# The last two experts' second products left for the routing, with one expert's middle units parked in DRAM

## The chip, the cores and the metric

One core of one Trainium2 chip. TensorE multiplies, VectorE, ScalarE and GpSimd work on elements, SP issues most transfers; each engine takes its instructions in the order in which the program gives them, and waits on semaphores for the others. The metric is the time of one launch in device microseconds.

## The reference

The reference runs a windowed attention, a layer of four weighted experts and a layer of eight experts with a fixed capacity, over 1536 tokens of 512 features.

```python
def _moe_ref(x, domain_probs, w1, w2):          # E = 4, F = 1024
    p = domain_probs / (domain_probs.sum(-1, keepdims=True) + 1e-09)
    ...
    for e in range(E):
        h = np.maximum(x @ w1[e], 0.0)
        out += p[:, e:e + 1] * (h @ w2[e])

def _moe2_ref(x, w_gate, w1, w2):               # E = 8, cap = N // E = 192
    logits = x @ w_gate
    flat = logits.flatten()
    order = np.argsort(-flat)
    ...
    for idx in order:
        tok, e = (int(idx) // E, int(idx) % E)
        if assigned[tok] >= 0 or counts[e] >= cap:
            continue
        assigned[tok] = e
        counts[e] += 1
    ...
    for e in range(E):
        mask = assigned == e
        h = np.maximum(x[mask] @ w1[e], 0.0)
        out[mask] = h @ w2[e]
```

A token's expert in the second layer depends on the rank of its logit among all tokens of that expert, so ranks must be exact over all 12288 logits.

## The kernel before

Tokens come in 12 blocks of 128. Every float32 operand is split into two float16 parts, high and low, and a product is three float16 products. The hidden layer stands with its units on partitions, so a first product (`g1`, 12 matmuls a step) needs no transpose after it.

The program has four stages. `phase1` (0 to 352 us) does the attention and experts 0 and 1, in an order written out as a list (`ORDER1`). `phase3` does expert 2 ("mid") and the first product of expert 3 ("last"), unit by unit: unit m holds blocks 2m and 2m+1. For each unit, `a00` to `a31` are the eight steps of mid's first product and `a40` to `a71` those of the last expert's; `r` is the relu out of the accumulators, `h` the high part and `l` the low part of the result. Mid's parts go into one pair of buffers (`HH`), the last expert's over the tokens themselves (`xTall`, high) and into `hl3` (low), which both stay until the routing. `s00` to `s17` are mid's second products for units 0 to 4 (`KEEP = 5`), added into `y` by `add`.

The logits of the second layer are not taken from the finished `y`. `norm`, `sc`, `xh`, `xl`, `row` split a block of `y` as far as it is summed, SP transposes it, and `log_mm` adds to its product with the gate the products of kept hidden units with `gv`, which is W2 times the gate (made by `gate_of`: `turn` transposes W2, `prod` multiplies, `gate` closes). So an expert's second product may be done after the logits. Here this holds for the last expert in all blocks and for mid in blocks 10 and 11.

Ranking runs beside it, block by block (`lm`, `lo`, `rr`, `cm`, `rc`, `ct`, `rk`): `rank_rows` turns the block's logits into rows, `compare` (VectorE) compares each of the 8 experts' logits of this block with all blocks up to it, `row_count` (ScalarE) sums along rows, `count` (TensorE) along columns, `ranked` puts the two together. In blocks 8 to 11 two experts are summed on VectorE instead of ScalarE. Ties within the block are taken off by a second instruction with the mask `notbefore`.

Second products left over are cut into fills of two matmuls each (`defer`): 2 blocks of mid and 12 of the last expert, 14 x 12 = 168 fills. `side_step`, called after every third fill, does what follows a finished block: add, square, scale, high, low, and the write of the row to DRAM (`rows`). `FILLS` puts 75 of them into phase 3; the routing (`route`), a chain of 30 hops between VectorE and TensorE, calls `HOPS[i]` fills ahead of hop i; what is left runs after it, three fills to a step of `pump`, which loads, scales and splits the second layer's weights.

The order of phase 3 comes from due times: `TIMES3` within a unit, plus `PERIOD3` for each unit, `RANK` and `FILLS`, sorted (`ORDER3` is empty). The second layer gathers rows of 192 tokens an expert from DRAM (`gather`, an indirect transfer of GpSimd), transposes them (`gather_T`) and runs the experts.

```python
            while fills:
                fill(3)
                s.pump(1)
            while s.side:
                s.side_step()
                s.pump(1)
            W = s.finish(2, 0)
            big.close()
```

## Time and profile before

| | us |
|---|---|
| median of 3 runs (870.05 to 871.53) | 871.49 |
| the profiled execution | 871.92 |
| its span, first to last instruction | 870.1 |
| TensorE busy | 769.3 |
| VectorE busy | 612.3 |
| ScalarE busy | 494.4 |
| GpSimd busy | 244.7 |

Times in the rows are microseconds from the start of the span. The page gives each engine's busy tenths in 40 slices; a stretch can be asked for with the busy time of each engine in it, and with the granted clock of TensorE as a share of 2.4 GHz (1.00 is 2.4, 0.50 is 1.2). A matmul's duration includes its way through the array, so matmuls that follow each other overlap: what one costs is the distance from its start to the next start.

### The profile page before, as it was taken

Reading aid. Unit: us, or ns where it says so; the run is one execution under the profiler, and the core shown is the slowest. Engines: PE = TensorE matmul, PEld = TensorE weight load, DVE = VectorE, ACT = ScalarE, POOL = GpSimd, SP = SyncE. Lnnn points to the kernel's source line nnn. Section 1 sums busy time; section 2 is a strip of 40 time slices with the busy share of each in tenths; the row PEclk is TensorE's granted clock in tenths of the full one; section 3 lists DMA queues with packets and bytes.
Section 4 is the critical chain, followed back from the end, with each engine's and each line's share of the span. In section 5 each row is a group of like instructions: output and inputs, shape, how many; then the busy total and the mean of one; then the engine's idle time right before and its main releaser. Section 6 shows DMA issues by size and latency. Waiting matters only on the chain. (4 is left out here: it accounts for less than half of the span.)

```text
span 870.1 us, 21221 instructions
## 1 busy us (share of the span) xinstructions
PE 769.3 (88%) x8660; PEld 591.3 (68%) x8664; DVE 612.3 (70%) x1545; ACT 494.4 (57%) x989; POOL 244.7 (28%) x287
## 2 busy tenths in 40 slices
PE   3688999999999999999999998889899147998996
PEld 3567767777776767768778685745344047898996
DVE  5998988767663543436668788999777545797790
...
PEclk9699999999999999999999999989999568999999
...
GB/s 281 254 193 131 150 157 160 127 133 59 98 111 171 98 68 80 109 98 14 26 2 26 14 24 23 48 69 1 183 37 39 132 221 336 257 256 331 177 38 38
DMA packets 191425, 103.75 MB, mean 119 GB/s; under 512 B 162272, under 2 KB 162272, under 8 KB 191328
## 3 DMA queue, kind: packets, MB, share of 16 engines
...
q8 instruction: 68, 1.11, 0.5%
...
## 5 line engine op out<-in xcount | busy, mean ns | idle before, releaser
L873 PEld LDWEIGHTS <-w 128*128 128x128 f16 x3456 | 246.5, 98 | 37.4 <-issue 5.4
L873 PE MATMUL pH<-xT,w 128*128 128x128 f16 (+1 forms) x3168 | 249.1, 234 | 3.7 <-ACT H L847 2.7
L884 PE MATMUL pY<-w,hh 128*128 128x512 f16 x544 | 161.7, 379 | 0.0
L884 PE MATMUL pY<-w,hl 128*128 128x512 f16 x272 | 103.1, 379 | 0.2 <-DVE hl L1425 0.2
L1017 ACT ACTIVATE Cj<-C 128x128 bf16<-128x128 bf16 (+11 forms) x88 | 75.3, 855 | 42.5 <-DVE C L1004 41.6
L1278 PEld LDWEIGHTS <-w 128*128 128x128 f16 x768 | 66.7, 102 | 37.0 <-DMA xg<-g 23.4
L847 ACT ACTIVATE H<-pH 128x512 f32<-128x512 f32 (+1 forms) x82 | 45.4, 559 | 61.9 <-PE pH L873 48.8
L1004 DVE TENSOR_SCALAR C<-w,Lg 128x1024 bf16<-128x1024 f32 (+7 forms) x112 | 72.2, 661 | 3.7 <-PE pw L1023 1.8
L1278 PE MATMUL pH<-xg,w 128*128 128x192 f16 x528 | 51.8, 259 | 22.0 <-DMA xg<-g 19.5
L884 PEld LDWEIGHTS <-hh 128*128 128x128 f16 x544 | 47.0, 98 | 33.6
L1298 PE MATMUL pR<-hh,w 128*128 128x192 f16 x512 | 64.9, 246 | 0.0
L1298 PEld LDWEIGHTS <-w 128*128 128x128 f16 x768 | 63.4, 98 | 1.9 <-issue 1.8
L1298 PE MATMUL pR<-hl,w 128*128 128x192 f16 x256 | 63.0, 246 | 0.0
L1049 PE MATMUL pY<-w,xT 128*128 128x512 f16 x192 | 60.4, 389 | 0.0
L569 POOL TENSOR_SCALAR hh<-H 128x512 f16<-128x512 f32 x40 | 28.5, 713 | 101.2 <-ACT H L847 76.0
L749 ACT ACTIVATE t<-pS,mx,ec 128x256 f32<-128x256 f32 (+1 forms) x96 | 51.6, 542 | 2.2
L764 POOL TENSOR_TENSOR pp<-t,pp 128x512 f16<-128x512 f32 (+1 forms) x34 | 39.8, 1175 | 44.4 <-ACT pp L567 36.0
L481 DVE SCALAR_TENSOR_TENSOR w<-w,wsr,w 128x1024 f16<-128x1024 f32 x32 | 40.3, 1279 | 13.4 <-ACT w L567 13.4
L1425 POOL TENSOR_TENSOR hl<-H,hh 128x512 f16<-128x512 f32 x26 | 32.9, 1267 | 56.4 <-DVE hh L571 31.7
L884 PEld LDWEIGHTS <-hl 128*128 128x128 f16 x272 | 26.5, 98 | 32.7 <-DVE hl L1425 0.7
L481 DVE SCALAR_TENSOR_TENSOR w<-raw,wsr,w 128x1024 f16<-128x1024 f32 x32 | 40.2, 1279 | 7.5 <-ACT w L567 7.2
L1049 PE MATMUL pY<-w,hl 128*128 128x512 f16 x112 | 44.2, 395 | 0.0
...
## 6 DMA issues: line engine op xcount, KB each, us to landing
...
rows<-xs SPq DMA_DIRECT2D x12, 260.0 KB, 2.7
x<-in_k_dram SPq DMA_DIRECT2D x12, 256.0 KB, 3.5
x<-in_q_dram SPq DMA_DIRECT2D x12, 256.0 KB, 4.3
```

Source lines behind the costliest of these rows:

```text
L481: V.scalar_tensor_tensor(l, r[:, d2], sc, h, op0=OP.mult, op1=OP.subtract)
L749: s.nc.scalar.activation(t[:, hh], ps[:, hh], AF.Exp, bias=mx[:, 1, hh:hh + 1], scale=e[:, 0:1], accum_out=s.SU[j][:, 2 * g + hh:2 * g + h ...
L764: (G if eng == "G" else V).tensor_sub(pl[:, x], t, ph[:, x])
L847: s.nc.scalar.activation(H, ps, AF.Relu, scale=HS)
L873: nc.tensor.matmul(o[f], w[:, d, 128 * (f0 + f):128 * (f0 + f) + 128], x[:, :, c], start=(d == 0 and i == 0), stop=(d == 3 and i == 2))
L884: nc.tensor.matmul(py, l[:, f], w[:, f], start=(f == 0 and i == 0), stop=(f == 7 and i == 2))
L1004: V.tensor_scalar(C[:, 8 * i:8 * i + n], x[:, :n, e], l, None, op0=OP.is_ge)
L1017: s.nc.scalar.activation(x, C, AF.Copy, accum_out=s.AC[j][:, 1, e:e + 1])
L1049: nc.tensor.matmul(py, a[:, f], w[:, f], start=(n == 0), stop=(n == 23))
L1278: nc.tensor.matmul(ps[0][:, f % 2], w[:, d, 128 * f:128 * f + 128], xg[:, :, c], start=(k == 0), stop=(k == 11))
L1298: nc.tensor.matmul(ps[0][:, d % 2], w[:, f, 128 * d:128 * d + 128], h[:, f], start=(k == 0), stop=(k == 23))
L1425: (nc.gpsimd if eng == "G" else nc.vector).tensor_sub(x[1], P.pop((e, j, c)), x[0])
```

## The change

Mid's second products leave phase 3 altogether: `second`, `s00` to `s17` and `add` go, and all 12 blocks of mid become fills, after the 12 of the last expert (288 fills). Since mid's buffers hold one unit only, `spill` writes each unit's two parts to DRAM, and when the last expert's fills of a block are done, the block's parts are read back over its own places in `xTall` and `hl3`. `log_mm` takes mid's hidden units for every block. A block's row steps now follow mid's fills, and the logits' split takes `y` with experts 0 and 1 alone.

In the ranking, `compare` covers the j blocks before the own one; the own block is one more instruction with the mask `lower`, whose result stands in `C` as block j and is counted like the others. The fixed part of the rank comes from `behind`. The accumulators are cleared in blocks 8 to 11 only. The shares `pe` are made at once for 12 blocks (`shares`). `FILLS` has 96 entries, `HOPS` 101 fills instead of 88, `junk` has a buffer of its own, and the whole order of phase 3, with the engine of each relu and part, is written out in `ORDER3` (775 steps; 18 of 48 relus, 29 of 48 low parts and 7 of 48 high parts on VectorE, 30 relus and 28 high parts on ScalarE).

```diff
-ORDER3 = """""".split()
-PERIOD3 = 35.0
+ORDER3 = """
+    norm0 sc0 a00 pump pump.1 mturn0 a01 pump.2 mturn1 a10 pump.3 pump.4 pump.5 pump.6 r0/A mprod0 a11 r1/V a20 mturn2
+    mturn3 mprod1 a21 mturn4 xh0/V h0/G pump.7 l0/G pump.8 pump.9 a30 mturn5 a31 xl0 r2/V h1/V a40 row0 l1/G r3/A
+    pump.10 pump.11 pump.12 pump.13 h2/G pump.14 mprod2 norm1 a41 pump.15 a50 pump.16 mturn6 a51 pump.17 sc1 mturn7
+    l2/G mprod3 xh1/V a60 a61 mgate start h3/A turn0 l3/G turn1 prod0 turn2 r4/A turn3 turn4 a70 a71 xl1 r5/A h4/A
...
+    xh1.1/A a70.1 r4.1/V a71.1 h4.1/A r5.1/V xl1.1 l4.1/V rc5.1 row1.1 a00.2 fill.3 rc6.1 h5.1/G norm0.2 ct5.1 r6.1/V
+    l5.1/G a01.2 sp.1 h6.1/G a10.2 r7.1/V fill.4 l6.1/V sc0.2 h7.1/G l7.1/V lm.2 a11.2 xh0.2/A lo.2 ct6.1 rr.2 r0.2/V
+    xl0.2 r1.2/A cm0.2 lm.3 fill.5 rc0.2 cm7.1 ct0.2 rc7.1 cm1.2 fill.6 ct7.1 h1.2/G row0.2 cm2.2 fill.7 cm3.2 norm1.2
+    a20.2 rk.1 rc1.2 lo.3 rc2.2 ct1.2 ct2.2 fill.8 fill.9 cm5.2 cm4.2 a21.2 rc3.2 sc1.2 rc4.2 ct3.2 h0.2/G rc5.2 a30.2
+    l0.2/V cm6.2 ct4.2 r2.2/A ct5.2 l1.2/V rc6.2 fill.10 cm7.2 rr.3 ct6.2 a31.2 cm0.3 cm1.3 r3.2/V rc7.2 rc0.3 ct7.2
...
+    rc2.11 rk.10 ct1.11 ct2.11 cm3.11 ct3.11 cm4.11 cm5.11 rc4.11 rc5.11 cm6.11 fill.74 fill.75 fill.76 fill.77
+    fill.78 fill.79 ct4.11 ct5.11 rc6.11 fill.80 fill.81 fill.82 fill.83 ct6.11 fill.84 fill.85 fill.86 fill.87 cm7.11
+    fill.88 fill.89 ct7.11 fill.90 rk.11 fill.91 fill.92 fill.93 fill.94 fill.95
+""".split()
+PERIOD3 = 29.0
...
-KEEP = 5
...
-HOPS = [0, 1, 3, 1, 7, 0, 3, 1, 7, 1, 3, 1, 7, 1, 3, 1, 7, 1, 3, 1, 7, 1, 4, 1, 7, 0, 3, 2, 4, 7]
+HOPS = [0, 1, 4, 1, 8, 1, 4, 1, 8, 1, 4, 1, 8, 1, 4, 1, 8, 1, 4, 1, 8, 1, 4, 1, 8, 1, 4, 1, 4, 7]
...
         V.tensor_copy(s.identh, s.identb)
-        s.notbefore = c.tile([128, 128], BF, name="notbefore")
-        V.tensor_scalar(s.notbefore, d0, 0.0, None, op0=OP.is_le)
+        s.lower = c.tile([128, 128], BF, name="lower")
+        V.tensor_scalar(s.lower, d0, 0.0, None, op0=OP.is_gt)
+        s.behind = c.tile([128, 1], F32, name="behind")
+        V.tensor_scalar(s.behind, d0[:, 0:1], -1.0, 127.0, op0=OP.mult, op1=OP.add)
         s.upper = c.tile([128, 128], BF, name="upper")
...
         xs, inv = s.XN.pop(j)
-        xt = s.xp.tile([128, 8, 128], F16, name="xt3" if j == s.NB - 2 else "xt2", bufs=1)
+        xt = s.xp.tile([128, 8, 128], F16, name=f"xt{2 + j % 2}", bufs=1)
         s.nc.sync.dma_start_transpose(xt, xs[:, 0:1024])
...
         s.AC[j] = s.sm.tile([128, 3, s.E2], F32, name="acc")
-        nc.vector.memset(s.AC[j][:, 2], 0.0)
+        if j >= 8:
+            nc.vector.memset(s.AC[j], 0.0)
         c = 64 + 128 * (j % 2)
-        s.PC[j] = s.pw[:, c:c + 8 * j].rearrange("p (a b) -> p a b", b=8) if j else None
+        s.PC[j] = s.pw[:, c:c + 8 * j + 8].rearrange("p (a b) -> p a b", b=8)
...
         C = s.Cs[j, e] = s.rk.tile([128, s.NB, 128], BF, name="C", bufs=3)
+        acc = s.on_dve(j, e)
         for i, x in enumerate(s.LR):
-            n = min(j + 1 - 8 * i, 8)
-            if s.on_dve(j, e):
+            n = min(j - 8 * i, 8)
+            if n < 1:
+                continue
+            if acc:
                 V.tensor_scalar(C[:, 8 * i:8 * i + n], x[:, :n, e], l, 0.0, op0=OP.is_ge, op1=OP.add,
...
-
-        jk = s.rk.tile([128, 128], BF, name="jk")
-        V.scalar_tensor_tensor(jk, s.LRof[j][:, e], l, s.notbefore, op0=OP.is_equal, op1=OP.mult,
-                               accum_out=s.AC[j][:, 0, e:e + 1])
+        kw = dict(accum_out=s.AC[j][:, 0, e:e + 1]) if acc else {}
+        V.scalar_tensor_tensor(C[:, j], s.LRof[j][:, e], l, s.lower, op0=OP.is_ge, op1=OP.mult, **kw)
...
         C = s.Cs.pop((j, e))
-        for jj in range(j):
+        for jj in range(j + 1):
             s.nc.tensor.matmul(s.PC[j][:, jj, e:e + 1], C[:, jj], s.ones[:, 0:1], start=True, stop=True)
...
         acc = s.AC.pop(j)
-        V.scalar_tensor_tensor(R[:, j], acc[:, 1], late, acc[:, 0], op0=OP.add, op1=OP.subtract)
-        V.tensor_add(R[:, j], R[:, j], acc[:, 2])
-        if j:
-            V.tensor_sub(R[:, :j], R[:, :j], s.PC.pop(j))
+        V.scalar_tensor_tensor(R[:, j], acc[:, 1], late, s.behind.to_broadcast([128, 8]), op0=OP.add, op1=OP.add)
+        if j >= 8:
+            V.tensor_add(acc[:, 0], acc[:, 0], acc[:, 2])
+            V.tensor_add(R[:, j], R[:, j], acc[:, 0])
+        V.tensor_sub(R[:, :j + 1], R[:, :j + 1], s.PC.pop(j))
         s.prefer(j)
+    def shares(s, e, W):
+        pe = s.cp.tile([128, s.NB], F32, name=f"pe_{e}")
+        s.nc.vector.scalar_tensor_tensor(pe, s.p[:, :, e], W[4], s.tsc, op0=OP.mult, op1=OP.mult)
+        s.kpe[e] = {j: pe[:, j:j + 1] for j in range(s.NB)}
...
             py = s.pys[e, j]
-            h, l = s.kept[e][j]
+            h, l = s.xTall[:, j], s.hl3[:, j]
             for n in (2 * k, 2 * k + 1):
...
             if k == 11:
-                s.side.append([add] if e < s.E1 - 1 else [add, norm])
+                s.side.append([add, norm] if e < s.E1 - 1 else [add])
+                if e == s.E1 - 1:
+                    for p, x in enumerate((s.xTall, s.hl3)):
+                        nc.sync.dma_start(x[:, j], s.spill[p, j])
...
-        NB, V, G, E = s.NB, s.nc.vector, s.nc.gpsimd, s.E2
-        ev, B, HH, PE, W3 = {}, {}, {}, {}, []
+        nc, NB, V, G, E = s.nc, s.NB, s.nc.vector, s.nc.gpsimd, s.E2
+        ev, B, HH, W3 = {}, {}, {}, []
         mid = s.E1 - 2
...
                     HH[m] = [s.hp.tile([128, 8, 2, 128], F16, name=x, bufs=1) for x in ("hh", "hl")]
-                    if m >= KEEP:
-                        pe = s.pe_of(mid, W[4], 2 * m, 2 * m + 2)
-                        for b in range(2):
-                            s.kept[mid][2 * m + b] = [x[:, :, b] for x in HH[m]]
-                            s.kpe[mid][2 * m + b] = pe[:, b:b + 1]
+                    for b in range(2):
+                        s.kept[mid][2 * m + b] = [x[:, :, b] for x in HH[m]]
                 h, l = [y[:, 2 * k:2 * k + 2] for y in HH[m]]
...
-        def second(m, b, i):
-            j = 2 * m + b
-            if m not in PE:
-                PE[m] = s.pe_of(mid, W[4], 2 * m, 2 * m + 2)
-            if i == 0:
-                B[j] = s.g2(W, HH[m][0][:, :, b], HH[m][1][:, :, b], j, PE[m][:, b:b + 1], False)
-            B[j][0][i]()
+        def spill(m):
+            for p in range(2):
+                nc.sync.dma_start(s.spill[p, 2 * m:2 * m + 2].rearrange("b q f t -> q f b t"), HH[m][p])
...
         W2 = s.gate_of(mid, W)
+        s.shares(mid, W)
...
                 at(f"r{k}", m, T, relu, m, k, after=rp + [(f"l{k - 2}", m) if k > 1 else (f"l{k + 6}", m - 1), (f"r{k - 1}", m)], eng="A")
-                at(f"h{k}", m, T, hid, m, k, 0, after=[(f"r{k}", m), ("a71", m) if k > 3 else ("s17", m - 1)], eng="G")
+                at(f"h{k}", m, T, hid, m, k, 0, after=[(f"r{k}", m)] + ([("a71", m)] if k > 3 else [("lm", 2 * m - 2), ("lm", 2 * m - 1), ("sp", m - 1)]), eng="G")
                 at(f"l{k}", m, T, hid, m, k, 1, after=[(f"h{k}", m)], eng="G" if k > 3 else "V")
-            y = [(f"l{k}", m) for k in range(4)]
+            at("sp", m, T, spill, m, after=[(f"l{k}", m) for k in range(4)])
             for b in range(2):
                 j = 2 * m + b
-                d = "" if m < KEEP else "d"
-                for i in range(8 if m < KEEP else 0):
-                    at(f"s{b}{i}", m, T, second, m, b, i, after=y + [(f"add{b}", m - 1)])
-                    y = [(f"s{b}{i}", m)]
-                if m < KEEP:
-                    at(f"add{b}", m, T, lambda j=j: B.pop(j)[1](), after=y)
-                xs = (("row1", m - 1) if b else ("row1", m - 2)) if d else ("row0", m) if b else \
-                    ("drow0", m + 1) if m + 1 == KEEP else ("row1", m - 1)
-                at(f"{d}norm{b}", m, T, norm, j, after=[(f"add{b}", m), xs])
-                at(f"{d}sc{b}", m, T, put, j, s.rows_scale, after=[(f"{d}norm{b}", m)])
-                at(f"{d}xh{b}", m, T, lambda e, j=j: s.rows_hi(s.XN[j], e), after=[(f"{d}sc{b}", m)], eng="G")
-                at(f"{d}xl{b}", m, T, put, j, s.rows_lo, after=[(f"{d}xh{b}", m)])
-                at(f"{d}row{b}", m, T, s.log_rows, j,
-                   after=[(f"{d}xl{b}", m), ("drow0" if d and not b else "lm", j - 2 if d else j - 1)])
+                at(f"norm{b}", m, T, norm, j, after=[("row0", m) if b else ("row1", m - 1)])
+                at(f"sc{b}", m, T, put, j, s.rows_scale, after=[(f"norm{b}", m)])
+                at(f"xh{b}", m, T, lambda e, j=j: s.rows_hi(s.XN[j], e), after=[(f"sc{b}", m)], eng="G")
+                at(f"xl{b}", m, T, put, j, s.rows_lo, after=[(f"xh{b}", m)])
+                at(f"row{b}", m, T, s.log_rows, j, after=[(f"xl{b}", m), ("lm", j - 2)])
         cs = []
...
             m, T = r // 2, PERIOD3 * (r // 2 + 1)
-            at("lm", r, T + RANK[4 * r + 0], s.log_mm, r, after=[(f"row{r % 2}", m), (f"drow{r % 2}", m), ("lo", r - 1), ("gate", 0)] + [(f"l{k}", m) for k in range(4, 8)])
+            at("lm", r, T + RANK[4 * r + 0], s.log_mm, r, after=[(f"row{r % 2}", m), ("lo", r - 1), ("gate", 0)] + [(f"l{k}", m) for k in range(8)])
             at("lo", r, T + RANK[4 * r + 0], s.log_out, r, after=[("lm", r)])
...
         at("gate", 0, 0, gate, after=[("prod3", 0)])
-        m = NB // 2 - 1
-        f = [("add0", m), ("add1", m), ("add0", m - 1), ("add1", m - 1)] + [(f"l{k}", m) for k in range(8)]
         for i, t in enumerate(FILLS):
-            ev["fill", i] = [PERIOD3 * m + t, fill, f + [("fill", i - 1)]]
+            j = i // 12
+            ev["fill", i] = [PERIOD3 * (NB // 2 - 1) + t, fill, [("fill", i - 1), ("gate", 0), (f"xl{j % 2}", j // 2), ("lm", j)]]
         for i, t in enumerate(PUMPS3):
...
             rows = dr.tile([s.N, ROW], F16, name="rows")
+            s.spill = dr.tile([2, NB, 128, 8, 128], F16, name="spill")
             s.rows = rows[:]
...
                     s.rk = pool(ph, "rk", 1, **re)
+                    s.shares(last, W)
                     for j in range(NB):
-                        pe = s.cp.tile([128, 1], F32, name=f"pe3_{j}")
-                        nc.vector.scalar_tensor_tensor(pe, s.p[:, j, last:], W[4], s.tsc[:, j:j + 1],
-                                                       op0=OP.mult, op1=OP.mult)
-                        s.kpe[last][j] = pe
                         s.kept[last][j] = (s.xTall[:, j], s.hl3[:, j])
-                    for j in range(2 * KEEP, NB):
-                        fills.extend(s.defer(last - 1, Wm, j))
                     for j in range(NB):
                         fills.extend(s.defer(last, W, j))
+                    for j in range(NB):
+                        fills.extend(s.defer(last - 1, Wm, j))
                 s.phase3(W, w1, open_rk, fill)
...
                 if s.nfill == 16:
-                    s.junk = s.y[:, 0:2].bitcast(F16).rearrange("p a (b f) -> p (a b) f", f=512)
+                    s.junk = pool(hb, "junk1", 1, **re).tile([128, 4, 512], F16, name="junk")
                 s.pump(1)
```

## Rows read from the trace of the kernel before

**Rows 1.** The page's 40 slices: TensorE's busy tenths and clock.
```profile
PE   3688999999999999999999998889899147998996
PEclk9699999999999999999999999989999568999999
```

**Rows 2.** Busy by stretch: length, PE, PEld, DVE, ACT, POOL, clock, DMA, GB/s.
```profile
458.30:496.40 38.10, 36.61 (x383) 28.26 (x381) 31.19 (x100) 21.65 (x50) 12.18 (x14) 1.00 0.08 15
496.40:534.40 38.00, 36.94 (x403) 28.72 (x401) 32.76 (x94) 23.69 (x49) 13.07 (x15) 1.00 0.17 22
562.10:617.50 55.40, 46.47 (x501) 25.32 (x498) 52.65 (x163) 33.22 (x53) 8.91 (x16) 0.94 0.17 57
617.50:678.70 61.20, 55.33 (x399) 24.27 (x397) 44.37 (x155) 22.92 (x44) 1.03 (x10) 0.95 0.20 76
678.70:707.20 28.50, 0.51 (x4) 0.29 (x5) 17.34 (x29) 16.40 (x20) 4.25 (x4) 0.50 0.55 151
```

**Rows 3.** Timeline, TensorE, routing: start, us, line, operation, count.
```profile
639.75 0.59 PE L1049 MATMUL pY<-w,xT 128*128 128x512 f16 x2
...
640.40 0.59 PE L1049 MATMUL pY<-w,xT 128*128 128x512 f16 x2
```

**Rows 4.** Timeline of TensorE in unit 2: logit, count and first products.
```profile
426.43 0.17 PE L957 MATMUL pq<-gv,hl 128*128 128x8 f16 x1
426.46 0.16 PE L1023 MATMUL pw<-ones,C 128*128 128x1 bf16 x1
426.48 1.47 PE L873 MATMUL pH<-xT,w 128*128 128x256 f16 x12
427.79 0.17 PE L1023 MATMUL pw<-ones,C 128*128 128x1 bf16 x1
```

**Rows 5.** Groups by line and shape, 380 to 617: count, busy us, mean ns.
```profile
L1004 DVE TENSOR_SCALAR C<-w,Lg 128x1024 bf16<-128x1024 f32 x32 | 25.3, 790 | 0.1
...
L1004 DVE TENSOR_SCALAR C<-w,Lg 128x512 bf16<-128x512 f32 x14 | 7.6, 543 | 0.0
...
L1007 DVE DVE_READ_ACCUMULATOR jk<-w,Lg,notbefore 128x1 f32 x96 | 7.6, 79 | 0.0
...
L891 DVE SCALAR_TENSOR_TENSOR y<-pY,pe,y 128x512 f32<-128x512 f32 x10 | 7.5, 745 | 21.0 <-PE pY L884 20.9 <-PE pw L1023 0.2
...
L567 ACT ACTIVATE xs<-y,rgr 128x512 f16<-128x512 f32 x2 | 1.4, 714 | 1.3 <-DVE rgr L324 1.3
```

**Rows 6.** Busy time in the first stage, columns as in rows 2.
```profile
40.00:100.00 60.00, 52.79 (x785) 43.69 (x784) 56.17 (x124) 48.41 (x124) 30.33 (x27) 0.96 0.78 170
```

**Rows 7.** Timeline, start of unit 1: TensorE and SP's queue.
```profile
376.84 0.59 PE L884 MATMUL pY<-w,hh 128*128 128x512 f16 x2
...
380.79 1.25 SPq L919 DMA_TRANSPOSE wtl<-w  x1
```

**Rows 8.** DMA issues: line, count, KB each, us to landing.
```profile
rows<-xs SPq DMA_DIRECT2D x12, 260.0 KB, 2.7
x<-in_k_dram SPq DMA_DIRECT2D x12, 256.0 KB, 3.5
```

**Rows 9.** Timeline of TensorE in the routing: products of two rounds, the last one.
```profile
642.65 0.46 PE L1179 MATMUL pq<-v,D 128*8 128x40 bf16 x12
...
649.64 0.46 PE L1179 MATMUL pq<-v,D 128*8 128x40 bf16 x12
...
674.78 0.71 PE L1237 MATMUL pq<-gt,Coh 128*96 128x16 f16 x12 [1.77 <-DVE Coh L1232]
```

**Rows 10.** The chain that ended last, in order of time: two weight loads.
```profile
680.42 5.59 DMA w<-in_moe_w_dram
...
690.47 5.97 DMA w<-in_moe_w_dram
```

**Rows 11.** Timeline after the routing: first gather, second layer's first product.
```profile
698.15 1.13 POOL L1247 DMA_INDIRECT g<-rows,idx  x1 [24.25 <-DMA rows<-xs]
...
707.04 5.13 PE L1278 MATMUL pH<-xg,w 128*128 128x192 f16 x39 [18.73 <-DMA xg<-g]
```

109 lines of the change are left out of this document (57 added, 52 removed), and 5 rows, old and new, of the table FILLS.

## The prediction

> **What bounds the kernel now.** Read the slices first [rows 1]: counted from 0, TensorE is full from slice 4 to slice 23, then at 8 or 9 tenths, and in slices 31 to 33 (674 to 740 us) at 1, 4 and 7, with clock digits 5, 6 and 8. Then ask for stretches [rows 2]. In two units of the last experts' stage (a unit is two token blocks, numbered from 0; these are 3 and 4) TensorE is busy 36.6 of 38.1 and 36.9 of 38.0 us, while VectorE works 31 to 33: TensorE's order sets the pace. After the last first product (562.1) VectorE is busy 52.65 of 55.4: the ranking's compares set it. The routing (617.5 to 678.7) has TensorE at 55.3 of 61.2, filled by deferred products. Then 28.5 us with TensorE at 0.51 busy, at the lower clock. So four stretches have three limits, and the change trades between them.
>
> **Prices.** Three 512-column matmuls of a second product start 0.65 us apart as a set, so 24 cost 24 x 0.216 = 5.2 and one fill (two matmuls) 0.432 us [rows 3]. A step of a first product (12 matmuls) is 1.31 us, from 426.48 to 427.79; the logit and count matmuls cost about 0.025 each, their 0.17 being overlapped [rows 4].
>
> **Part 1, second products out of the stage.** Ten products of the middle expert leave (52 us of TensorE); fills in the stage go from 75 to 96 (+9.1). Logits now take the middle units for all blocks: 10 x 16 = 160 matmuls more, and the own block's count adds 96: 6.4 us together. Along the written order, TensorE's content of units 1 to 5 up to their last first product is 16 x 1.31 plus logits 2.1, 16 transposes about 1.7 (an estimate at the 0.109 us of a 256-column matmul, 1.31/12), counts 0.4 to 3 and 3, 8, 9, 4 and 4 fills: 26.9, 29.5, 30.6, 29.3 and 29.7, together 146.0 us.
> VectorE no longer has slack beside that. Compares over j blocks instead of j+1 telescope: each expert loses one 1024-wide compare (0.79) over blocks 0 to 7, and one 512-wide (0.543) over 8 to 11 [rows 5]: 8 x (0.79 + 0.543) = 10.7 us. The own block by a mask stays one instruction of the same width; 88 accumulator reads of 0.079 go, 7.0 us. Ten adds of 0.745 move later. Against that the logits' sum gains 10 x 0.4 us, and the order gives VectorE 18 of the 48 relus, none before (at some 0.7 each, as other 512-wide operations, 12.6 us). So unit 3's 31.2 us [rows 2] becomes 31.2 - 1.5 (adds) - 3 (a sixth of the 17.7 saved) + 2 to 3 = 29 to 30: as full as TensorE. ScalarE's 21.7 gains a sixth of 28 high parts of 0.71 us: about 25.
> How close can a written order come with two engines full? In the first stage, from 40 to 100 us, VectorE is busy 56.17 of 60 (0.936), TensorE 52.8, ScalarE 48.4 [rows 6]. I take 0.94 of the fuller engine; the bounds are 0.88, TensorE's share in that row, and 0.97, TensorE's in unit 4 [rows 2].
> Unit 0 still starts at 352.7. Its first products end at 377.0, after which the old order ran second products [rows 7]. Now unit 1's product and the last expert's gate products follow. The last transpose for them is issued at 380.79 and lands some 3 us later (2.7 to 3.5 in [rows 8]), at 384, and the fourth gate product stands before the third step of unit 1, which could start at 381: 1.5 + 3.5 us of waits that 10.4 us of second products hid. Units 1 to 5: 146.0 / 0.94 = 155.3, so the last first product ends at 537.3 (before 562.1).
> The tail is VectorE's: 52.65 less three compares already done (24 to 21, some 1.6 each with the mask), 1.9 for narrower compares, 1.3 for accumulator reads, plus 2 for parts that come after 537: about 47; at 0.94, 50. The routing starts at 587.3 instead of 617.5: **30.2 us earlier**.
>
> **Part 2, spill and reload.** Twelve writes of 512 KB in pieces of 256 B, and 24 reloads of 256 KB, all on SP's queue. Each unit's write must land before the next unit's first high part overwrites the buffer, and behind it in that queue stand the row transposes. Loads of 256 KB in such pieces land after 3.5 us, row writes of 260 KB after 2.7 [rows 8]; two writes of twice the size: 6 (overlapped) to 14 us (in sequence). The last low part of a unit's middle expert is ready some 15 us before the unit ends, and the next unit's first high part stands after six of its steps, 8 us: I take nothing, with up to 3 us a unit if the write is issued only behind the last row transpose. A reload has over 100 fills before its reader: nothing; without that cover it would be 3 us each.
> The Trainium skill ("DMA: Bandwidth & Descriptors", Specifications) says that below 512 B a transfer turns into read-modify-write. No write of such pieces to DRAM stands in this trace; if that doubles the landing, it is the last rival below.
>
> **Part 3, routing.** Before, 168 fills: 75 in the stage, 88 in the 30 hops, 5 after. Now 288: 96, 101 and **91 after**. The hops last from 617.5 to 675.5 = 58 us, one round 6.96 us [rows 9], of which 12 fills are 5.2: TensorE leads. 13 more fills are 5.6 us; of which I let 4.6 disappear: 88 fills are 38.0 us and the chain's own products some 9 (14 groups of 0.46 and smaller ones), so TensorE waits 11 of the 58, some of it where a fill is now added; and blocks become final later, so that fewer row steps (0.745 us each on VectorE) stand in the routing's way. Bounds 58 and 63.6; I take 59.0: the routing ends at 646.3. Then 91 x 0.432 = 39.3, with 1 for the queue: fills end at 687 instead of 678.7, **8 us later**.
>
> **Part 4, the gap.** Today 28.5 us lie between the last fill and the first product of the second layer [rows 2]. The chain of waits shows two weight loads of 5.6 and 6.0 us, each behind a split that frees its buffer; the last row write waits in the same order and is there only for the gather at 698.15, and TensorE resumes at 707.04, 8.9 us later [rows 10, 11]. Every three fills call one step of weight preparation: 31 steps under the 91 fills cover the loads and splits. What stays is the last block's chain: add, square, high and low of 512 columns at 0.71 to 0.75 each [rows 5], some 1.2 for small steps and waits between engines, the write's 2.7 [rows 8] and 0.7 to the gather, about 7.5 (twice the small steps and a write at 3.5 would make 9.5), then 8.9: **16.4 us, 12.1 less**. The second layer starts at 703.0 and runs as before (162.9): its loads follow the gather in both. TensorE is idle at the lower clock in either gap; I count no difference.
>
> **Sum** against the profiled execution (871.92; span 870.1): fills' end +8, gap -12.1, so -4.1: 867.8. The median of the runs is 871.49, 0.4 lower: I say **868**. So of 30 us won in the stage 22 come back as products after the routing: only work put under the old gap counts, and the sign hangs on idle TensorE time in the stage. The runs of before spread over 0.2%, about what a measurement here can tell; that is 1.7 us.
>
> **Rivals.**
> 1. *Three engines in one order wait for each other.* At 0.90 instead of 0.94 units and tail are (146 + 47)/0.90 = 214.4 instead of 205.3: +9.1, **877**, slower. It decides from 0.92 down, where the routing starts after 591. For it: ScalarE at 25 of 30 in the same units, single-buffered hidden parts, and no second products left that hide a late relu. Against: units 3 and 4 ran TensorE at 0.96 to 0.97 beside VectorE at 0.82 to 0.86.
> 2. *The order is as good as the units of today*, 0.97: 199.0, -6.3: **861.5**.
> 3. *The gap doesn't shrink*: preparation stalls on loads as now, or holds the adds back that free the two accumulators, and the 28.5 us follow 91 fills: +12.1, **880**. That would be the change not doing what its tail is laid out for. Against: 39 us are twice the loads' time.
> 4. *The spill is late*: 3 us in each of 5 units: **883**. For it the small pieces; against it a DMA share of 0.08 in unit 3 [rows 2].
>
> **How the numbers follow.** Forecast 0.45, between 862 and 873; rival 1 0.25, rival 2 0.17, rival 3 0.06, rival 4 0.07. Faster by over 0.2% (under 869.8): 0.29 of the forecast's chance and all of rival 2, 0.46. Slower (over 873.2): 0.02 of the forecast's, 0.22 of rival 1, rivals 3 and 4 less 0.01: 0.36. Within: 0.18. The range of 859 to 881 reaches rivals 1, 2 and most of 3 and leaves out the rest; the forecast's own is 862 to 873.
>
> **What would show it.** The trace of after should have the last first product near 537, the routing's first step near 587, fills ending near 687, TensorE resuming near 703; units of 31 to 33 us with TensorE at 0.94; compares on VectorE shorter by 11 us in sum; no high part waiting for a DMA write. A routing start after 591 with the gap at 16 is rival 1; fills that end at 687 and a resumption after 710 is rival 3. A second layer other than 162.9 us, or a new wait in the 91 fills, would break the sum in a place where I have no term.

## The result, and the profile after

| | before | after |
|---|---|---|
| median of 4 runs each, us | 871.51 (870.05 to 872.61) | 863.77 (861.97 to 864.41) |
| ratio, 95% interval | | 0.9909 (0.9887 to 0.9931) |
| profiled execution / its span, us | 871.92 / 870.1 | 861.97 / 860.2 |

The kernel is faster by 0.9%, 7.7 us. The forecast was 868, so the time lies between it and rival 2 (861.5), nearer to the rival. Laid out by the stretches of the forecast's sum, each end read as the first or last start of a line's instructions in the trace:

| stretch, us | before | forecast | after |
|---|---|---|---|
| up to unit 0 | 352.7 | 352.7 | 354.4 |
| unit 0, to unit 1's start | 36.1 | 29.3 | 26.8 |
| units 1 to 5 | 173.3 | 155.3 | 149.4 |
| tail, to the routing's first step | 55.4 | 50.0 | 47.4 |
| routing | 57.9 | 59.0 | 58.1 |
| fills behind the routing | 3.2 | 40.3 | 46.1 |
| gap, to the second layer's first product | 28.3 | 16.4 | 15.7 |
| second layer and end | 163.1 | 162.9 | 162.3 |

Two entries are off by more than 3 us, and they have opposite signs: units 1 to 5 are 5.9 us shorter than forecast, the fills behind the routing 5.8 us longer. The prediction's sign was right; of the 7.7 us it forecast 3.5. That the time itself came within 5 us is in part luck, since these two misses cancel. The 1.7 us of the first entry are spread: the same first stage took 352 to 357 us in the profiled executions below.

The page's slices of after; the two rows answer to [rows 1]:

```profile
PE   3688999999999999999999999979998757999996
PEclk9689999999999999999999999989999869999999
```

The hole before the second layer (counted from 0, slices 31 to 33) had 1, 4 and 7 tenths; it is now 8, 7, 5 and 7 tenths in slices 30 to 33: shallower, not gone. Busy time by stretch, columns as in [rows 2] (length, PE, PEld, DVE, ACT, POOL, clock, DMA share, GB/s), for units 3, 4 and 5, the tail, the routing, the fills behind it and the gap:

```profile
441.00:471.50 30.50, 30.50 (x388) 26.13 (x385) 27.67 (x79) 21.66 (x53) 3.08 (x4) 1.00 0.22 49
471.50:501.30 29.80, 29.66 (x412) 26.02 (x409) 27.59 (x75) 26.19 (x53) 4.19 (x4) 1.00 0.46 100
501.30:530.60 29.30, 29.30 (x408) 26.04 (x406) 27.74 (x75) 25.19 (x48) 4.85 (x5) 1.00 0.06 11
530.60:578.00 47.40, 41.64 (x493) 24.00 (x491) 44.30 (x138) 29.01 (x44) 5.52 (x13) 0.93 0.31 85
578.00:636.10 58.10, 56.52 (x417) 25.61 (x416) 37.33 (x139) 11.37 (x16) 0.00 (x0) 1.00 0.39 137
636.10:682.20 46.10, 41.53 (x186) 18.11 (x184) 24.64 (x46) 26.67 (x51) 0.98 (x9) 0.96 0.31 104
682.20:697.90 15.70, 0.02 (x1) 0.00 (x0) 7.98 (x11) 5.19 (x7) 4.37 (x4) 0.62 0.48 121
```

TensorE works through units 3 to 5 almost without a visible pause (29.3 of 29.3 us in the last, with VectorE at 27.7 and ScalarE at 25.2). The tail is still VectorE's, 44.3 of 47.4. In the routing TensorE's visible idle time is down to 1.6 us. Then, in the stretch that did not exist before, 4.6 of 46.1 us are idle, at a granted clock of 0.96. That is the term the forecast did not have.

What TensorE and the others wait for in that stretch (engine, line waited for; us in total, times, longest):

```profile
DVE w L494 <- ACT w L580: 8.7, 4, 4.9
...
PE pY L1072 <- DVE y L1086: 4.6, 3, 2.0
...
ACT junk L469 <- DMA w<-in_moe_w_dram: 4.5, 2, 3.0
```

and the timeline of one of the three stops (start, us, engine, line; in brackets the wait before it):

```profile
647.19 1.91 ACT L469 ACTIVATE junk<-w 128x2048 f16<-128x2048 f32 x1 [1.54 <-DMA w<-in_moe_w_dram]
...
649.10 2.17 ACT L580 ACTIVATE w<-w,wsr 128x1024 f16<-128x1024 f32 x2
...
650.26 1.28 DVE L494 SCALAR_TENSOR_TENSOR w<-w,wsr,w 128x1024 f16<-128x1024 f32 x1 [4.93 <-ACT w L580]
651.46 0.75 DVE L1086 SCALAR_TENSOR_TENSOR y<-pY,pe,y 128x512 f32<-128x512 f32 x1
...
652.26 0.59 PE L1072 MATMUL pY<-w,xT 128*128 128x512 f16 x2 [2.04 <-DVE y L1086]
```

Read from the bottom: TensorE waits 2.04 us for an add that frees an accumulator; the add stands on VectorE behind a weight's low part, before which VectorE stood idle for 4.93 us until ScalarE's high part; ScalarE was busy with a sum of squares, and that had waited for a weight load to land. Here a DMA stops TensorE through the queues of two other engines, with no dependence between the two ends. The other long stop, at 664.83, comes 7.8 us after the other wait for a load, along the same engines with row steps in between; the short one, 0.5 us at 644.88, has no such wait ahead of it. This is the second half of rival 3 ("holds the adds back that free the two accumulators"), at 5 us and without the gap.

VectorE's ranking, 350 us to the routing (line, operation, shapes, count | busy us, mean ns), before:

```profile
L1004 DVE TENSOR_SCALAR C<-w,Lg 128x1024 bf16<-128x1024 f32 (+7 forms) x112 | 72.2, 661 | 3.7 <-PE pw L1023 1.8 <-ACT Cj L1017 1.0 <-ACT w L987 0.7
L1007 DVE SCALAR_TENSOR_TENSOR jk<-w,Lg,notbefore 128x128 bf16<-128x128 f32 x96 | 41.8, 436 | 0.0
...
L1001 DVE TENSOR_SCALAR_CACHE_REDUCE C<-w,Lg 128x1024 bf16<-128x1024 f32 (+4 forms) x16 | 13.9, 903 | 0.0
```

and after:

```profile
L1022 DVE TENSOR_SCALAR C<-w,Lg 128x1024 bf16<-128x1024 f32 (+7 forms) x98 | 58.8, 615 | 0.6 <-PE pw L1039 0.4 <-ACT Cj L1033 0.2
L1024 DVE SCALAR_TENSOR_TENSOR C<-w,Lg,lower 128x128 bf16<-128x128 f32 x96 | 36.5, 383 | 1.9 <-PE pw L1039 1.1 <-ACT w L1000 0.6
L1019 DVE TENSOR_SCALAR_CACHE_REDUCE C<-w,Lg 128x1024 bf16<-128x1024 f32 (+3 forms) x14 | 12.6, 928 | 0.0
```

Compares fall by 13.4 + 1.3 us (forecast 10.7), the own block by 5.3 (forecast nothing, since its instruction keeps its width); the accumulator reads of 7.6 us [rows 5] shrink to 8 of some 0.08: 7.0, as forecast. Together 27 us where the forecast had 17.7. About 19 of them come with the ranking's edit itself: with the old ranking in after's order (e2 below) the groups sum to 128.9 us, against 109.6 in after and 136.7 in before. The rest comes with the new order and engines.

The gap, in the chain that ended last (start, us, what): from the last block's scale to the gather's landing.

```profile
684.48 0.50 DVE xs L584
...
685.00 0.76 DVE xs L1120
...
685.89 2.02 DMA rows<-xs
...
688.83 1.61 POOL g L1274
...
693.19 3.96 DMA g<-rows,idx
```

No weight load stands in it any more, where before two did [rows 10]. The last row write is shorter too: in before it was issued at 691.26, 0.8 us behind the second of these loads, and landed 5.9 us later; here it landed after 2.0 (that the load ahead of it is the reason is not tested). From the first gather to the second layer's first product it is 9.1 us, 688.8 to 697.9, before 8.9 [rows 11].

The spill (line's tiles, count, KB each, median us from issue to landing):

```profile
spill<-hh SPq DMA_DIRECT2D x6, 512.0 KB, 4.4
spill<-hl SPq DMA_DIRECT2D x6, 512.0 KB, 6.0
xT<-spill SPq DMA_DIRECT2D x12, 256.0 KB, 2.6
hl<-spill SPq DMA_DIRECT2D x12, 256.0 KB, 3.0
```

4.4 and 6.0 us are for 512 KB in pieces of 256 B. Where the trace tells the landing of the second write, both had landed 6.7 to 7.8 us after the first was issued, near the lower of the two figures taken for the pair, 6 and 14, and 2.4 us or more before the next unit's first high part. The read-modify-write below 512 B that the Trainium skill states ("DMA: Bandwidth & Descriptors", Specifications) may or may not happen, which no run here shows; a doubled landing is not in these rows.

### The profile page after: what moved, and what is told of

Same layout as the page of the kernel before. It is cut to its first block, busy times and chain, and to the rows that moved or that the text cites. A ratio compares the mean times of both kernels' runs of the same rounds, so it can differ in the third digit from the quotient of the medians.

```text
span 860.2 us, 21736 instructions
## 1 busy us (share of the span) xinstructions
PE 777.3 (90%) x8916; PEld 600.1 (70%) x8920; DVE 608.4 (71%) x1467; ACT 502.2 (58%) x1004; POOL 206.4 (24%) x238
## 5 line engine op out<-in xcount | busy, mean ns | idle before, releaser
L886 PE MATMUL pH<-xT,w 128*128 128x128 f16 (+1 forms) x3168 | 252.9, 235 | 2.2 <-ACT H L860 1.6
L1072 PE MATMUL pY<-w,xT 128*128 128x512 f16 x384 | 120.7, 386 | 4.6 <-DVE y L1086 4.6
L897 PE MATMUL pY<-w,hh 128*128 128x512 f16 x384 | 114.7, 381 | 0.0
L1033 ACT ACTIVATE Cj<-C 128x256 bf16<-128x256 bf16 (+11 forms) x88 | 75.3, 855 | 28.2 <-DVE C L1024 21.6
L860 ACT ACTIVATE H<-pH 128x512 f32<-128x512 f32 (+1 forms) x70 | 38.4, 554 | 55.1 <-PE pH L886 34.4
L1072 PEld LDWEIGHTS <-xT 128*128 128x128 f16 x384 | 36.5, 99 | 42.1 <-issue 8.6
L1022 DVE TENSOR_SCALAR C<-w,Lg 128x1024 bf16<-128x1024 f32 (+7 forms) x98 | 58.8, 615 | 0.6 <-PE pw L1039 0.4
L777 POOL TENSOR_TENSOR pp<-t,pp 128x512 f16<-128x512 f32 (+1 forms) x34 | 40.1, 1183 | 44.4 <-ACT pp L580 35.9
L584 DVE TENSOR_SCALAR hh<-H 128x384 f16<-128x384 f32 (+1 forms) x53 | 20.9, 396 | 37.5 <-ACT H L860 37.0
L897 PEld LDWEIGHTS <-hh 128*128 128x128 f16 x384 | 32.9, 98 | 19.6
L469 ACT ACTIVATE junk<-w 128x2048 f16<-128x2048 f32 x16 | 30.5, 1906 | 25.4 <-DMA w<-in_moe_w_dram 25.4
```

The lines of the kernel that those rows point to most:

```text
L469: A.activation(x, s.raws[k, q][0], AF.Square, accum_out=J["ss"][:, q:q + 1])
L777: (G if eng == "G" else V).tensor_sub(pl[:, x], t, ph[:, x])
L860: s.nc.scalar.activation(H, ps, AF.Relu, scale=HS)
L886: nc.tensor.matmul(o[f], w[:, d, 128 * (f0 + f):128 * (f0 + f) + 128], x[:, :, c], start=(d == 0 and i == 0), stop=(d == 3 and i == 2))
L897: nc.tensor.matmul(py, l[:, f], w[:, f], start=(f == 0 and i == 0), stop=(f == 7 and i == 2))
L1022: V.tensor_scalar(C[:, 8 * i:8 * i + n], x[:, :n, e], l, None, op0=OP.is_ge)
```

## The experiments

Each edit is to the kernel after, except in the two that say before. The stretches are read as above, in us; the ratio is to the kernel before, on the same chip. The second layer takes 160 to 167 us in the profiled executions, also where its code is the same, and the first stage 352 to 357; that is most of the spread of the times. The stretches between them repeat within about 1 us (compare after and e12_after_again, but for the fills), so the verdicts rest on them.

| kernel | ratio (95%) | units 1 to 5 | tail | routing | fills behind | gap |
|---|---|---|---|---|---|---|
| before | 1 | 173.3 | 55.4 | 57.9 | 3.2 | 28.3 |
| after | 0.991 (0.989 to 0.993) | 149.4 | 47.4 | 58.1 | 46.1 | 15.7 |
| e1_by_time | 1.109 (1.103 to 1.115) | 215.3 | 70.4 | 60.7 | 44.3 | 15.7 |
| e10_old_engines | 1.005 (1.002 to 1.008) | 157.4 | 50.8 | 58.0 | 44.4 | 15.7 |
| e2_old_ranks | 1.003 (1.001 to 1.005) | 157.4 | 51.4 | 58.0 | 46.5 | 15.8 |
| e3_mask_alone (before) | 0.999 (0.996 to 1.002) | 173.5 | 54.8 | 55.6 | 2.2 | 28.8 |
| e4_no_spill | 0.985 (0.980 to 0.990) | 150.0 | 46.9 | 58.1 | 46.2 | 15.7 |
| e7_old_hops | 0.986 (0.981 to 0.991) | 149.9 | 48.0 | 54.6 | 45.0 | 15.7 |
| e8_more_hops | 0.984 (0.978 to 0.989) | 150.2 | 48.4 | 63.7 | 35.2 | 15.7 |
| e5_prep_behind | 0.991 (0.988 to 0.994) | 150.2 | 48.2 | 58.0 | 39.3 | 19.2 |
| e6_landed | 0.983 (0.977 to 0.988) | 150.2 | 48.3 | 58.1 | 40.1 | 15.5 |
| e9_before_late (before) | 1.005 (1.002 to 1.007) | 173.0 | 55.4 | 49.3 | 15.2 | 24.7 |
| e11_landed_again | 0.986 (0.982 to 0.990) | 150.2 | 48.3 | 58.1 | 40.1 | 15.9 |
| e12_after_again | 0.989 (0.985 to 0.993) | 150.2 | 48.2 | 58.0 | 44.5 | 15.8 |

### What the written order is worth: e1_by_time

```diff
-ORDER3 = """ norm0 sc0 a00 pump ... """.split()
+ORDER3 = """""".split()
```

> The kernel after, but the last experts' stage in the order of the table of times instead of the written order; the work itself stays. Theory A, the order makes the engines fit (the written order reached TensorE busy 148.2 of 149.4 us in units 1 to 5 with VectorE at 127.6 and ScalarE at 101.6): in a rough order the three wait for each other, at the lower bound of the prediction, 0.88, units 1 to 5 and the tail take (146 + 47)/0.88 = 219 us against the measured 196.8, so about 886 us, slower than the kernel before. Theory B, the content sets the time, since TensorE has most of it: 0.94 as forecast, 205 us, so 872 us, equal to before. Rival: the order is worth nothing, 864 us.

Units 3 and 4 of it, and its tail (columns as in [rows 2]):

```profile
479.30:526.80 47.50, 32.24 (x375) 27.14 (x375) 26.23 (x77) 21.52 (x52) 11.26 (x14) 0.86 0.17 34
526.80:574.00 47.20, 33.45 (x393) 28.40 (x393) 26.24 (x71) 22.18 (x47) 11.34 (x14) 0.83 0.17 35
...
612.40:682.80 70.40, 59.30 (x549) 30.96 (x546) 50.79 (x145) 29.58 (x42) 7.87 (x17) 0.83 0.15 46
```

Every theory was far too low: 94 us slower than before on the same chip, 104 slower than after on another, at the same work. The edit takes more than the order: the engine names stand in the order, so relus and parts go back to the old engines as in e10 below, which differs from e1 in the order alone and whose span is 91.7 us shorter (873.3 against 965.0). The table's due times of the ranking (`RANK`) are still before's, so this prices one rough table, not the best one. No engine is full; TensorE stops 46.7 us in units 1 to 5 for compares and rank sums that its tiny count matmuls need, and the granted clock falls to 0.83 to 0.86 in stretches with such stops, so that its own matmuls take longer too (32.2 us busy where after has 30.5 in unit 3). That before ran well by such a table, with second products between the counts, fits this but was not tried apart. With this table, the order is not a refinement of the change but a part of it.

### Which part of the order: e10_old_engines

```diff
-    ... r0/A mprod0 a11 r1/V a20 ... xh0/V h0/G ... l4/V ...
+    ... r0 mprod0 a11 r1 a20 ... xh0 h0 ... l4 ...
```

> The kernel after with the written order kept, but every relu on ScalarE, every high part on GpSimd, and the low parts on GpSimd or VectorE as in before (the engine names taken out of the order). Theory A: the order alone carries the units, TensorE leads, and the slower GpSimd lies in its shade: units 1 to 5 within 3 us of 149.4 in sum, 864 to 867 us. Theory B: the split over three engines is what fits the units into 30 us; GpSimd's parts of 0.7 and 1.2 us stand in places written for 0.4 to 0.75, ScalarE has 18 relus more (1.8 us a unit), so 1.5 to 4 us a unit come on top: 872 to 885 us, slower than before.

Units 3 and 4 and the tail:

```profile
442.40:476.60 34.20, 32.58 (x388) 27.64 (x386) 25.27 (x70) 20.52 (x48) 11.10 (x15) 0.95 0.16 39
476.60:510.20 33.60, 31.55 (x416) 27.20 (x413) 29.05 (x72) 22.91 (x47) 11.75 (x15) 0.95 0.42 91
...
539.70:590.50 50.80, 42.70 (x492) 24.28 (x491) 47.03 (x142) 29.04 (x43) 8.67 (x18) 0.93 0.29 79
```

Theory B. Units 1 to 5 come 8.0 us later than in after, the tail 3.4, and the whole gain is gone (1.005). Against the forecast's content of 146.0 us this is 146.0/157.4 = 0.93, a little under the forecast's 0.94; after has 146.0/149.4 = 0.98, a little over rival 2's 0.97. So rival 1's mechanism, engines in one order that wait for each other, is real and costs 11.4 us here, though the engine waited for is a fourth one, GpSimd: TensorE stops 4.4 us in units 1 to 5 before logit products that need GpSimd's low parts, where after has no such stop, and its busy time is 3.9 us longer, with a granted clock of 0.95 in three of the five units. What the engine names do is to take work from GpSimd: it has 10 to 12 us in units 2 to 5 of e10 and 3 to 6 in after, and parts of 0.7 to 1.2 us go to ScalarE and VectorE at 0.4 to 0.8.

### What the ranking is worth: e2_old_ranks and e3_mask_alone

In after the ranking is put back, in before it is put in alone:

```diff
-            n = min(j - 8 * i, 8)
+            n = min(j + 1 - 8 * i, 8)
...
-        V.scalar_tensor_tensor(C[:, j], s.LRof[j][:, e], l, s.lower, op0=OP.is_ge, op1=OP.mult, **kw)
+        V.scalar_tensor_tensor(jk, s.LRof[j][:, e], l, s.notbefore, op0=OP.is_equal, op1=OP.mult,
+                               accum_out=s.AC[j][:, 0, e:e + 1])
```

> The kernel after with the ranking's compares as before: own block within the wide compare, and a second instruction of 128 columns whose sum goes through an accumulator read; 17.7 us more on VectorE. Theory A, VectorE shares the units: 12 blocks share the 17.7, about 3 us a unit, so units 3 to 5 hold 30.7 us of VectorE beside 29.7 of TensorE and take 31.5 instead of 29.9 (+1.6 each, +5), and the tail with two to three blocks of compares +3.5 (47.4 to 51): about 872 us. Theory B, TensorE alone sets the units: +3.5 in the tail, 867 us. Rival: a fixed order turns every us of VectorE into waiting, +12 or more, 876 us and slower than before.

> The kernel before with the new ranking alone (own block by a mask, 17.7 us less on VectorE and 96 tiny matmuls more), nothing else changed. Theory A: its units are TensorE's (busy 36.9 of 38.0 us), so they stay or gain some tenths, and the tail, VectorE's, falls by the 3 to 4 us of two to three blocks' compares: 868 us against 871.5. Theory B: units 3 to 5 waited for VectorE too and give 1 us each: 865 us, and so more than half of the change's gain is the ranking's. Rival: the order by the table of times reshuffles and nothing is won: 871 us.

In after the rival came: units 1 to 5 +8.0 and the tail +4.0 us, all of the gain. Unit 4 of e2_old_ranks:

```profile
472.80:506.50 33.70, 31.07 (x399) 26.84 (x396) 29.43 (x92) 26.60 (x55) 4.06 (x4) 0.95 0.42 92
```

Here VectorE works 1.8 us more than after's 27.6 and the unit is 3.9 longer, but unit 4 is the worst of the five. Over units 1 to 5 VectorE works 8.4 us more (135.9 against 127.5) and they take 8.0 longer; in the tail it is 3.2 and 4.0. So in this order a us more of VectorE's work costs about a us. In before the same edit takes 22 us from VectorE's ranking ahead of the routing (its groups sum to 136.7 there and to 114.6 in e3) and moves next to nothing there: units 173.5, tail 54.8 instead of 55.4. The routing behind it is 2.3 us shorter (55.6 against 57.9, its granted clock 1.00 against 0.97), and the ratio, 0.996 to 1.002, neither shows nor excludes so small a gain. The two largest groups of e3 show where VectorE's time went, and the last row is its tail; their waits for TensorE's counts, which free the compares' buffers, are 7.0 and 3.3 us, where before's rows above have 1.8 and none:

```profile
L1011 DVE TENSOR_SCALAR C<-w,Lg 128x1024 bf16<-128x1024 f32 (+7 forms) x98 | 62.6, 655 | 7.8 <-PE pw L1028 7.0 <-ACT Cj L1022 0.8
L1013 DVE SCALAR_TENSOR_TENSOR C<-w,Lg,lower 128x128 bf16<-128x128 f32 x96 | 37.5, 392 | 5.9 <-PE pw L1028 3.3 <-ACT Cj L1022 2.1 <-ACT w L989 0.5
...
565.00:619.80 54.80, 49.21 (x527) 26.49 (x523) 50.33 (x147) 33.16 (x53) 8.82 (x16) 0.88 0.19 68
```

So the forecast's reading that VectorE's busy time sets before's tail did not hold there: VectorE lost 2.3 us in it (50.3 against 52.65), the tail 0.6. The tail's granted clock fell as well, from 0.94 to 0.88, with TensorE busy for 49.2 us instead of 46.5; what of this held the tail is open. What e2 cannot tell is how much of its 12 us is VectorE's work as such and how much an order written for other durations.

### The spill: e4_no_spill

```diff
-            for p in range(2):
-                nc.sync.dma_start(s.spill[p, 2 * m:2 * m + 2].rearrange("b q f t -> q f b t"), HH[m][p])
...
-                    for p, x in enumerate((s.xTall, s.hl3)):
-                        nc.sync.dma_start(x[:, j], s.spill[p, j])
```

> The kernel after without the write of the middle units to DRAM and without their reload; the deferred products of the middle expert then read the last expert's units, so their values are not the reference's. Theory A, the spill is hidden (the prediction's nothing): 864 us, within 1.5 us. Rival 4 of the prediction, a high part waits for the write in each of 5 units: each us of such a wait comes back, up to 15 us, under 860 us. A third reading: no wait in the units, but the 24 reloads on the same queue as the routing's and the weights' loads delay those: 1 to 3 us less after the routing, 861 to 863 us.

Units, tail, routing and fills are those of after within 0.6 us each. The spill costs nothing in any of them, and rival 4 falls. The ratio is 0.6% lower, with an interval that meets after's. Nothing in the stretches where the spill works stands behind that, and the profiled execution (866.2 us) is the slowest of the four, so what does stays open.

### The fills: e7_old_hops and e8_more_hops

```diff
-HOPS = [0, 1, 4, 1, 8, 1, 4, ...]
+HOPS = [0, 1, 3, 1, 7, 0, 3, ...]    # e7: 88 in all
+HOPS = [0, 1, 4, 1, 9, 1, 5, ...]    # e8: 114 in all
```

> The kernel after with the 88 fills of before in the routing's 30 pauses instead of 101 (13 fills, 5.6 us of TensorE, go behind the routing). Theory A, the chain of VectorE's hops sets the routing below some 100 fills (TensorE's visible idle time in it was 5.9 us before and 1.6 us in after): the routing stays within 1 us of 58.1 and the 13 fills add 5.6 behind it: 869 us, 5 slower than after. Theory B, TensorE sets it: the routing gets 5.6 shorter, the time behind it 5.6 longer: 864 us. The prediction's 4.6 of 5.6 lies with A.

> The kernel after with 114 fills in the routing's pauses instead of 101. Theory A: only 1.6 us of idle TensorE is left there, so 13 fills more lengthen the routing by 4 to 5.6 us and take 5.6 to 6.2 from behind it (fewer fills, and with them part of the stops): 863 us, 0 to 2 us under after. Theory B: the pauses still hide fills, the routing stays at 58 to 59: 859 us. Rival: with 78 fills left, fewer steps of preparation run under them and the gap gets longer: 865 us or more.

The routing and the fills behind it, of e7 and then of e8:

```profile
580.40:635.00 54.60, 51.28 (x391) 23.17 (x389) 36.23 (x136) 12.50 (x16) 0.00 (x0) 1.00 0.41 145
635.00:680.00 45.00, 45.00 (x212) 20.24 (x210) 25.33 (x49) 25.54 (x51) 0.99 (x9) 1.00 0.31 107
```

```profile
577.50:641.20 63.70, 62.12 (x443) 28.15 (x442) 40.01 (x143) 14.06 (x23) 0.22 (x2) 1.00 0.37 133
641.20:676.40 35.20, 33.93 (x160) 15.15 (x158) 21.73 (x43) 23.71 (x43) 0.76 (x7) 1.00 0.33 117
```

Neither theory of e7 holds alone: 13 fills fewer shorten the routing by 3.5 of their 5.6 us, 13 more lengthen it by 5.6, the full price. So 2.1 us, not 4.6, of the 13 added fills disappeared in the pauses. Routing and fills together are 99.6 and 98.9 us against 104.2 in after: both lost after's stops but for 1.2 us, presumably since another number of fills shifts the loads against the adds. With it their times, 859.8 and 858.1 us, lie under every theory's. In e7 104 fills run in 45.0 us = 0.433 each, with all the weight preparation beside them.

### The stops: e6_landed, then e11_landed_again beside e12_after_again

```diff
+            if q < 2 and s.filling and not s.landed(k, q):
+                continue
             if q < 4:
...
+            s.filling, s.wait = True, 6
             while fills:
```

> The kernel after, with one rule more under the 91 fills: ScalarE's sum of squares of a weight is only queued six preparation steps after its load was issued, so that ScalarE does not stand before a load that has not landed (4.5 us of such waits in two places in after). Theory A: these waits hold the high part, that the low part on VectorE, that the add behind it, and so an accumulator; two of the three stops of TensorE go, the fills end 42 us after the routing instead of 46.1, the gap stays at 16: 860 us, 4 us under after. Rival: VectorE's and ScalarE's own work holds the adds (splits of 1.28 and 1.13 us in bursts), the stops stay and the gap gets longer by the steps that were put off: 864 to 868 us.

> The kernel of e6_landed once more, beside after on the same chip. Theory A (two stops of TensorE under the 91 fills, held by ScalarE's wait for a load, are gone for good): 5 to 7 us under after, fills end 40 to 41 us after the routing. Rival (the time of e6 was the spread between executions in the second layer, 160 to 167 us): 2 us or less under after.

> The kernel after, unchanged, on the same chip as e11_landed_again: 0.991 of before, about 863 us; its fills end 46 us after the routing, as in its first profile, if the stops are the order's and not chance; 40 to 42 us if they come and go from execution to execution.

The fills behind the routing in e6_landed:

```profile
636.00:676.10 40.10, 39.57 (x187) 17.67 (x184) 24.71 (x46) 26.62 (x51) 0.98 (x9) 1.00 0.35 120
```

Theory A: the same VectorE and ScalarE work (24.71 and 26.62 us against 24.64 and 26.67), only queued later, takes 46.1 down to 40.1 us, which is the forecast's 40.3, at a clock of 1.00. Of the 6.0 us, 4.0 are stops (4.6 less the one of 0.5, which stays) and 2.0 are TensorE's busy time, 41.5 us at a granted clock of 0.96 and 39.6 at 1.00. After once more (e12) has 44.5, between its two theories, with three stops of 3.0 in sum: their length varies, they don't vanish.

The chain in the timeline and this experiment agree, but a wait for a load does not make a stop by itself. In e7 ScalarE stands as long for two loads, and TensorE never stops:

```profile
ACT junk L469 <- DMA w<-in_moe_w_dram: 4.8, 2, 3.0
```

So such a wait makes a stop only where the add that it delays comes too late for TensorE, which depends on where the preparation stands among the fills. That e6 works by the waits that it takes away, and not by shifting the preparation as e7 does, is read from the timeline and not shown apart.

In runs on one chip e11 has 859.1 us against e12's 862.5, 3.3 less and so between its theory (5 to 7) and its rival (2 or less), with intervals that overlap (0.982 to 0.990 and 0.985 to 0.993); in the traces it is 40.1 + 15.9 against 44.5 + 15.8, 4.3 us. So a version with one rule more than after lies 1.4 to 1.8% under before.

### The gap: e5_prep_behind and e9_before_late

```diff
             while fills:
                 fill(3)
-                s.pump(1)
```

and, in before, 58 fills in the pauses instead of 88, so that 35 stand behind the routing:

```diff
-HOPS = [0, 1, 3, 1, 7, 0, 3, 1, 7, ...]
+HOPS = [0, 1, 2, 1, 4, 0, 2, 1, 4, ...]
```

> The kernel after, but no step of weight preparation is called under the 91 fills behind the routing; they come after the last fill, as before. Theory A, the forecast's: the preparation under the fills is what shrinks the gap, at the price of the adds it holds back. Without it the three stops of TensorE (0.5, 2.0, 2.0 us) are gone and the fills end 41 to 42 us after the routing instead of 46.1, but the gap goes back from 15.7 to about 28: 8 us slower than after, 872 us. Rival: the gap is the last block's chain and the gather's whatever is done, since the loads land early now; then the gap stays near 16 to 18 and the kernel is 3 us faster than after, 861 us.

> The kernel before with 58 instead of 88 fills in the routing's pauses, so that 35 instead of 5 stand behind it: the change's last part without its stage. Theory A: the gap shrinks here too, because with fills in front of it the last block's low part no longer stands on VectorE behind a split that waits for a load; routing 57.9 - 30 x 0.22 to 0.27 = 50 to 51 us, 35 x 0.432 = 15 to 16 us behind it, gap 16 to 19 us: 82 to 86 us from the routing's start to the second layer against 89.4 before, 864 to 868 us. Theory B: the routing is VectorE's chain and stays near 57, so that what the gap gives goes into the fills: 871 us, no change. Rival 3 of the prediction: the gap stays at 28: 877 us, slower.

e5_prep_behind, fills and gap:

```profile
635.50:674.80 39.30, 39.30 (x185) 17.79 (x182) 16.77 (x33) 16.70 (x41) 0.99 (x9) 1.00 0.28 95
674.80:694.00 19.20, 0.40 (x5) 0.11 (x2) 10.28 (x20) 11.24 (x14) 4.54 (x4) 0.62 0.50 149
```

91 fills alone take 39.3 us, the term to the tenth. But the gap goes back to 19.2, not to 28, which is nearer to the rival than to theory A: fills and gap are 58.5 us without preparation under the fills and 61.8 with it, so in after the overlap loses 3.3 us net up to the second layer. The whole time doesn't show that: the ratio is 0.991 for both. e9 is the other way round: preparation runs under its 35 fills, and the gap is 24.7 all the same. Its timeline shows what is in it (684.65 is the last block's add):

```profile
684.65 0.74 DVE L1059 SCALAR_TENSOR_TENSOR y<-pY,pe,y 128x512 f32<-128x512 f32 x1
685.67 1.91 ACT L456 ACTIVATE y<-w 128x2048 f16<-128x2048 f32 x1 [2.45 <-DMA w<-in_moe_w_dram]
...
692.67 0.75 DVE L1093 SCALAR_TENSOR_TENSOR xs<-y,rgr,xs 128x512 f16<-128x512 f32 x1
```

The last block's low part starts 8.0 us after that add: its squares stand on ScalarE behind a sum of squares that waited for a load, and after that its scale stands on VectorE behind another weight's low part. The same distance is 5.3 us in e5 (674.87 to 680.17), 2.75 in after (682.25 to 685.00) and 9.5 in before:

```profile
680.83 0.74 DVE L1059 SCALAR_TENSOR_TENSOR y<-pY,pe,y 128x512 f32<-128x512 f32 x1
...
690.37 0.75 DVE L1093 SCALAR_TENSOR_TENSOR xs<-y,rgr,xs 128x512 f16<-128x512 f32 x1
```

The gaps are 28.3 (before), 24.7 (e9), 19.2 (e5) and 15.7 (after), in the same order. Of the 12.6 us between before and after, 6.8 lie between that add and the low part, 4.0 between the low part and the gather (the row write's landing) and 2.1 ahead of the add, which comes 2.1 us after the last fill in before and at once in after. So the gap's length goes with what stands in ScalarE's and VectorE's queues ahead of the last block's few steps, a wait for a load above all, and for a third with the write's landing. For before itself 30 fills moved are worth nothing (82 to 86 us expected from the routing's start to the second layer, 89.2 measured, 89.4 before): the routing gave 8.6, the fills took 12.0, the gap gave 3.6. No theory of e9 had these three together, and by the times it is 0.5% slower than before.

## Why the prediction came out as it did

- **Units and tail.** TensorE's content was nearly right: 146.0 us forecast for units 1 to 5, 148.0 busy, run in 149.4. The step that was off is "0.94 of the fuller engine", taken from the first stage; it was 0.98. A term under it was mis-sized: VectorE's saving in the ranking was 27 us and not 17.7, and in units 3 to 5 VectorE works 27.6 to 27.7 us, not 29 to 30. Either the old engines (e10) or the old ranking (e2) brings 0.93 back, so 0.94 was a fair figure for an order with one of the two. In the tail the share held (44.3 of 47.4, 0.93) and VectorE's content was mis-sized, 44.3 for 47. ScalarE's "about 25" left out the 18 relus that go to VectorE; it was 21.7 in unit 3 and 26.2 in unit 4. The waits at unit 1's start were over-priced by some 2.5 us (TensorE waited 2.6 for the transposes).
- **Routing.** 59.0 against 58.1 is right, the mechanism half so. Added fills disappeared only to 2.1 us of 5.6 (e7), and further ones not at all (e8). The other effect named, fewer row steps in the routing's way, is the larger: with the 88 fills of before, after's routing is 54.6 against 57.9, with VectorE at 36.2 against 42.6 us. Before's routing holds 10 low parts of rows on VectorE, 7.3 us, and e7's none. The round "of 6.96 us" is 6.99 by [rows 9], which changes nothing.
- **Fills behind the routing.** 39.3 us for 91 is exact (e5). The term that was missing is 4.6 us of stops, and with them a granted clock of 0.96: 6.0 us against e6. It was in the rivals, as a cause why the gap would stay; it came in another place.
- **Gap.** 15.7 against 16.4. Its chain (last block's steps, write, gather, 9 us to the product) is as forecast. The reason given, 31 steps of preparation under the fills, is not the main one: 9.1 of the 12.6 us are won without them (e5). Preparation under fills alone did not shrink before's gap to the forecast's 16 either (e9: 24.7).
- **Spill.** Nothing, as forecast (e4).
- **Sum.** "Only work put under the old gap counts" was the wrong summary. Its "22 come back" is wrong by the forecast's own terms, by which 37 us come back as fills behind the routing (40.3 against 3.2); and its terms add up to 867.4, which was rounded up to 868. Measured against before, unit 0 to the tail gives 41.2 us, the fills behind the routing take 42.9, the gap gives 12.6: the sign does hang on the stage, and there on the written order (e1 against e10: 91.7 us), on the engines in it (e10) and on the new ranking (e2). Each of the three is worth the whole gain or more.
